# A DFT exchange through DRAM becomes a transposing DMA, for six of eight batches

## The chip, the cores and the metric

The kernel runs on one core of a Trainium2 chip. TensorE (PE, with its weight loads shown apart as PEld) multiplies, ScalarE (ACT) and VectorE (DVE) empty the PSUM banks and do the elementwise work, GpSimd (POOL) and SyncE (SP) issue most of the DMAs. The metric is the device time of one execution in microseconds (us), smaller being better. The kernel before takes 849.25 us, the median of three runs (849.11 to 849.75).

## The reference

Two steps follow each other. The first is a Fourier mixing layer, the second a two-layer network on every token:

```
x: (8, 3008, 256)                      # batch, sequence, dim
X  = rfft(x, axis=1)                   # along the sequence
Yr = Xr @ w_r - Xi @ w_i + b_r         # complex matmul over dim
Yi = Xr @ w_i + Xi @ w_r + b_i
Y  = sign(Y) * max(|Y| - 0.01, 0)      # real and imaginary part apart
y  = irfft(Y, n=3008, axis=1)
h  = y.reshape(24064, 256) @ w_in      # (256, 2048)
g  = s * max(h, 0)**2 + b
out = g @ w_out                        # (2048, 256), float32
```

## The kernel before, in words

The sequence length is factored as 3008 = 94 x 32 (n1 and n2). The Fourier transform is then two short transforms, both done as matmuls with tables: one over n1 (94 values in, 96 table columns out, table `A_t`), then one over n2 (32 values, table `F_t`) for pairs of n1-frequencies. The inverse goes the other way: `T_t` over n2, then `C_t` over n1.

Between the transform over n1 and the one over n2 the data must change its layout: the first has n1 on the partitions, the second wants (frequency, n2) on the partitions, 128 at a time. This is the first exchange. The inverse has a like one, the second exchange (`vd`, `vs`).

Work is cut into units, small pieces for each batch b:

- `s1_units(b)`: 16 units, the transform over n1. In each, one matmul with `A_t` as the weights (94 x 96) and 512 columns of `x16`, the batch's input in float16, moving (L549); one eviction of 96 x 512 to the tile `u` (L171 on ACT or L175 on DVE). After every fourth unit SP stores 384 KB to a DRAM tile `ud` (L556). After the last one SP issues four loads of 384 KB from `ud` into four tiles `us` (L563), now with the wanted layout.
- `s23_units(b)`: the transform over n2 from `us` (L585), the complex matmul (L600, L614), the threshold, the inverse over n2 (L644), a store of `v` to DRAM (`vd`, L653), and at the end two loads of 768 KB into the tiles `vs` (L660). On the way SP copies blocks inside a tile `ring` (L634), 40 DMAs a batch.
- `s4_units(b)`: 14 units, the inverse over n1 from `vs` (L697): in each up to five pairs of a weight load (96 x 128 of `vs`) and a matmul of 96 moving columns of `C_t`. The result `yt` is what the network reads.

The network is the main stream. Its tokens come in 48 tiles of up to 512, each with 16 slots. In a slot `first_mm` issues two matmuls of the tile with `w_in` (L748), ACT applies the relu (L755), DVE or ACT the square (L762, L759), and `second_mms` of the tile before follow with `w_out` (L819, about four matmuls of 256 columns a slot). Two blocks of 128 output rows share an `ost` buffer, filled by DVE (L829) and stored by SP; there are three such buffers.

`schedule(start, span, units)` spreads a batch's units over slots; the order in which the program emits them is the order of every engine's queue. With s0, s1, s2 the first slots of batches b-2, b-1 and b, `s1_units(b)` takes slots s0+40 to s1-8, `s23_units(b)` begins at s1+2, `s4_units(b)` takes s2-14 to s2-2. Batch 0 goes another way (`first_batch`), in which `first_mm` has no part yet: its transform over n1 has the data as weights and `A_t` moving, four pairs to a unit (L361), and needs no exchange. Batch 1 has its s1 units at the end of `first_batch`. The evictions are dealt to ACT and DVE by a running estimate of both loads (`evac`).

Buffers: `u` has three (`upool`), `us` five of a quarter of a batch each (`uspool`; the tables `F_c` and `F_2` of batch 0 use them first), `vs` two halves (`vspool`). `emit_load_x(b+1)` loads the next batch's input at slot s1+6 into the four `x16` buffers, once the s1 units have read the old one.

Of the kernel before, what the change touches and what calls it, by code (L numbers as in the profile page):

```python
# [9 lines left out]
F16 = mybir.dt.float16  # L10
# [4 lines left out]
P = 128  # L15
N1 = 94
N2 = 32
NPAIR = 24
# [78 lines left out]
def kernel(  # L97
# [13 lines left out]
    nc = tc.nc  # L111
    B, S, D = x.shape
# [35 lines left out]
    fpool = ctx.enter_context(tc.tile_pool(name="psf", bufs=2, space=bass.MemoryType.PSUM))  # L148
    dpool = ctx.enter_context(tc.tile_pool(name="dram", bufs=2, space=bass.MemoryType.DRAM))
    xpool = ctx.enter_context(tc.tile_pool(name="xp", bufs=4))  # L150
    upool = ctx.enter_context(tc.tile_pool(name="up", bufs=3))
    uspool = ctx.enter_context(tc.tile_pool(name="usp", bufs=5))
    xfpool = ctx.enter_context(tc.tile_pool(name="xfp", bufs=4))
    mpool = ctx.enter_context(tc.tile_pool(name="mp", bufs=2))
    vpool = ctx.enter_context(tc.tile_pool(name="vp", bufs=3))
    vspool = ctx.enter_context(tc.tile_pool(name="vsp", bufs=2))
    ypool = ctx.enter_context(tc.tile_pool(name="yp", bufs=2))
    tpool = ctx.enter_context(tc.tile_pool(name="tp", bufs=2))
    rpool = ctx.enter_context(tc.tile_pool(name="rp", bufs=3))
# [21 lines left out]
    def one_bank():  # L181
        return fpool.tile([P, 512], F32, name="psf", tag="psf")

    def other_bank():
        return apool.tile([P, 512], F32, name="psa", tag="psa")
# [43 lines left out]
    for r in (0, 64):  # L229
        for i, bv in enumerate((b_r, b_i)):  # L230
            nc.sync.dma_start(out=b_g[r : r + 1, i], in_=bv.unsqueeze(0))
    F_c = uspool.tile([P, H, 2, N2], F16, name="F_c", tag="us")
    F_2 = [uspool.tile([P, H, P], F16, name="F_2", tag="us") for _ in range(2)]
    b_h = cpool.tile([P, D], F16, name="b_h")
    nc.vector.memset(b_h, 0.0)

# [113 lines left out]
    def first_batch():  # L350
# [113 lines left out]
                ps.rearrange("p (k n) -> p n k", n=N2), 512,  # L464
            )

        for h in range(2):
            vs[(0, h)] = vspool.tile([96, HW, D], F16, name="vs", tag="vs")

        def turn(ec, k):  # L470
            ps = two_banks()
            for j in range(8):
                nc.tensor.matmul(
                    ps[0:96, j // 4, (j % 4) * P : (j % 4) * P + P],
                    vt[:, ec, 8 * k + j, :], eye_t, start=True, stop=True,
                )
            h, n = divmod(8 * k, HW)
            evac(
                vs[(0, h)][:, n : n + 8, ec * P : (ec + 1) * P],
                ps[0:96].rearrange("p h (j e) -> p (h j) e", e=P), 1024,  # L480
            )

# [2 lines left out]
        def last_dft(ec, n2):  # L485

            ps = [one_bank(), other_bank()]
            for j in range(8):
                h, k = divmod(n2 + j, HW)
                nc.tensor.matmul(  # L490
                    ps[j // 4][:, (j % 4) * 96 : (j % 4) * 96 + 96],
                    vs[(0, h)][:, k, ec * P : (ec + 1) * P], C_t,
                    start=True, stop=True,
                )
            for i in range(2):
                evac(
                    yt[:, ec, n2 + 4 * i : n2 + 4 * i + 4, :],
                    ps[i][:, 0:384].rearrange("p (j n) -> p j n", n=96), 384,
                )

        more = s1_units(1, True)

        def some(n):
            for _ in range(n):
# [31 lines left out]
        return more  # L536


    def s1_units(b, more_banks=False):

        ud = dpool.tile([96, N2, D], F16, name="ud", tag="ud")
        hold = {}

        def unit(i):
            c, j = divmod(2 * i, XCH)
            if j == 0:
                hold["u"] = upool.tile([P, XCH, D], F16, name="u", tag="u")
            ps = other_bank() if more_banks and i % 2 else one_bank()
            nc.tensor.matmul(  # L549
                ps[0:96, :], A_t[0:N1, :], x16[(b, c)][0:N1, j * D : (j + 2) * D],  # L550
                start=True, stop=True,
            )
            u = hold["u"]
            evac(u[0:96, j : j + 2, :], ps[0:96, :].rearrange("p (j d) -> p j d", j=2), 512)
            if j == XCH - 2:
                nc.sync.dma_start(  # L556
                    out=ud[:, c * XCH : (c + 1) * XCH, :], in_=u[0:96]
                )
            if i == N2 // 2 - 1:
                uv = ud.rearrange("k n d -> (k n) d").rearrange("(q p) d -> p q d", p=P)  # L560
                for q in range(4):
                    t = uspool.tile([P, 6, D], F16, name="us", tag="us")
                    nc.sync.dma_start(out=t, in_=uv[:, 6 * q : 6 * q + 6, :])  # L563
                    us[(b, q)] = t

        return [lambda i=i: unit(i) for i in range(N2 // 2)]

    def s23_units(b):
# [8 lines left out]
        def fwd_unit(i):  # L577

            bank = one_bank()
            ps = bank.rearrange("p (r c j k) -> p r c j k", r=2, c=DC, j=2)  # L580
            t = us[(b, i // 3)]
            for j in range(2):
                q = (2 * i + j) % 6
                for dc in range(DC):
                    nc.tensor.matmul(  # L585
                        ps[:, :, dc, j, :], t[:, q, dc * P : (dc + 1) * P],
                        F_t[:, 2 * i + j, :], start=True, stop=True,
                    )
            xt = xfpool.tile([P, 3, DC, P], F16, name="xf", tag="xf")
            evac(xt[:, 1:3].rearrange("p r c k -> p (r c k)"), bank, 512)  # L590
            nc.vector.tensor_tensor(out=xt[:, 0], in0=xt[:, 1], in1=xt[:, 2], op=ALU.add)
            load["dve"] += 0.25
            xf[i] = xt
# [46 lines left out]
        def inv_unit(i):  # L640
            ps = one_bank().rearrange("p (j e) -> p j e", j=2)
            z = zt.pop(i)
            for j in range(2):
                nc.tensor.matmul(  # L644
                    ps[:, j, :], T_t[:, 2 * i + j, :], z[:, j, :], start=True, stop=True
                )
            if i % 2 == 0:
                hold["v"] = vpool.tile([P, 4, D], F16, name="v", tag="v")
            v = hold["v"]
            h = 2 * (i % 2)  # L650
            evac(v[:, h : h + 2, :], ps, 512)
            if i % 2 == 1:
                nc.sync.dma_start(  # L653
                    out=vd[2 * i - 2 : 2 * i + 2].rearrange("q p e -> p q e"), in_=v
                )
            if i == H - 1:
                vv = vd.rearrange("q (k n) e -> (q k) (n e)", n=N2)
                for h in range(2):
                    t = vspool.tile([96, HW, D], F16, name="vs", tag="vs")
                    nc.sync.dma_start(  # L660
                        out=t.rearrange("k n e -> k (n e)"),
                        in_=vv[:, h * HW * D : (h + 1) * HW * D],
                    )
                    vs[(b, h)] = t

        units = []

# [14 lines left out]
    def s4_units(b):  # L682

        groups = []
        for lo in range(0, N2, 5):
            for ec in range(DC):
                groups.append((lo, min(5, N2 - lo), ec))

        def unit(g):
            n2, w, ec = groups[g]  # L690
            if g == 0:
                yts[b] = ypool.tile([P, DC, N2, 96], F16, name="yt", tag="yt")
            yt = yts[b]
            ps = one_bank()
            for j in range(w):
                h, k = divmod(n2 + j, HW)
                nc.tensor.matmul(  # L697
                    ps[:, j * 96 : (j + 1) * 96],
                    vs[(b, h)][:, k, ec * P : (ec + 1) * P], C_t,
                    start=True, stop=True,  # L700
                )
            evac(
                yt[:, ec, n2 : n2 + w, :],
                ps[:, 0 : w * 96].rearrange("p (j n) -> p j n", n=96), w * 96,
            )
            if g == len(groups) - 1 and b >= 2:
                pr, half = divmod(b, 2)
                if half == 0:
                    tails[pr] = tpool.tile([P, DC, 2, N2, 14], F16, name="tail", tag="tail")
                nc.gpsimd.tensor_copy(out=tails[pr][:, :, half], in_=yt[:, :, :, 80:94])  # L710

        return [lambda g=g: unit(g) for g in range(len(groups))]


# [127 lines left out]
    def schedule(start, span, units):  # L842
        for i, u in enumerate(units):
            plan.setdefault(start + (i * span) // len(units), []).append(u)
# [1 line left out]
    more = first_batch()  # L846
    load.update(act=0.0, dve=0.0)
    def load_x_2():
        emit_load_x(2, us[(1, 3)][0:1, 0, 0:1])

    mark = {}
    for i, tl in enumerate(tiles):
# [7 lines left out]
    for b in range(2, B):  # L860
        s0, s1, s2 = mark[b - 2], mark[b - 1], mark[b]
        p = s1 - s0
        schedule(s0 + 40, p - 48, s1_units(b))
        p = s2 - s1
        schedule(s1 + 2, p - 30, s23_units(b))
        schedule(s2 - 14, 12, s4_units(b))
        if b + 1 < B:
            plan.setdefault(s1 + 6, []).append(lambda b=b: emit_load_x(b + 1))
# [43 lines left out]
```

## Time and profile before

| what | value |
|---|---|
| time, median of three runs | 849.25 us |
| the profiled execution | 849.11 us |
| its span, first to last instruction | 847.2 us |
| TensorE clock granted | full in all slices |
| PE busy | 833.7 us, 98% |
| DVE busy | 691.5 us, 82% |
| ACT busy | 641.2 us, 76% |
| bytes moved by DMA | 96.06 MB, 113 GB/s |

The profile page gives busy time by engine, the span in 40 slices with the tenths of each that an engine was busy, the chain of work that ended last (followed back from the last instruction to what released it), and groups of instructions by line. In a group "out<-in" names the tiles, then come the shape, the count after "x", the busy time and the mean duration of one; behind the bar stands the idle time of the engine just before the group. A duration of a matmul holds its latency too, and matmuls overlap, so what one costs in a stream is read from the distance between starts in the timeline. Records of SP's queue are called SPq.

### The profile page before, as it was taken

How to read it: one execution, taken by the hardware profiler on the slowest of the kernel's cores; microseconds unless marked ns; L12 is line 12 of the kernel's file. 1: busy time of each engine (PE TensorE's matmuls, PEld its weight loads, DVE VectorE, ACT ScalarE, POOL GpSimd, SP SyncE). 2: the span in 40 equal slices, each digit the busy share in tenths (PEclk: the TensorE clock that was granted, in tenths of full speed). 3: DMA queues.
4: the chain of work that ended last, by engine and by line, in shares of the span. 5: the costliest groups of instructions: out<-in, count | busy, mean ns of one | idle time of the engine just before them, and what ended most of it. 6: DMA issues, size and time to landing. Idle time of an engine off the chain costs nothing.

```text
span 847.2 us, 17072 instructions
## 1 busy us (share of the span) xinstructions
PE 833.7 (98%) x6645; PEld 598.8 (71%) x6645; DVE 691.5 (82%) x1016; ACT 641.2 (76%) x854; POOL 45.6 (5%) x71
## 2 busy tenths in 40 slices
PE   7999999999999999999999999999999999999997
PEld 6757767777677766777677776777667777766765
DVE  5899987888878987888878888798977888776674
ACT  5888877787778877787777887787877777766673
POOL 4331000000000000000000000000000000000000
PEclk9999999999999999999999999999999999999999
DMA  8946467224762367324762248613354223411111
GB/s 200 173 131 139 118 160 192 78 70 108 193 161 60 99 157 191 95 79 108 179 173 57 73 105 202 170 41 91 101 156 120 61 79 98 112 33 39 38 44 50
DMA packets 105746, 96.06 MB, mean 113 GB/s; under 512 B 9542, under 2 KB 97482, under 8 KB 104322
## 3 DMA queue, kind: packets, MB, share of 16 engines
q1 hardware_dynamic: 99218, 80.55, 32.9%
q0 software_dynamic: 6448, 14.42, 10.5%
q8 instruction: 52, 0.85, 0.4%
q14 instruction: 28, 0.23, 0.1%
HBM read 53.52 MB, written 46.66 MB: 118 GB/s over the span
## 4 chain that ended last, share of the span: by engine, by line
PE 87%; DVE 4%; ACT 3%; DMA 3%; issue 2%; SPq 0%; POOL 0%; DVEq 0%; ACTq 0%; POOLq 0%
PE psa L819 36%; PE psh L748 35%; PE psf L614 4%; PE psf L549 2%; PE psf L600 2%; PE psf L585 2%; PE psf L644 2%; PE psf L697 2%; ACT rt L755 1%; DVE gt L762 1%; DMA out_dram<-ost 1%; DMA x<-in_x_dram 1%; DMA us<-ud 1%; DMA F_c<-dft_fwd 1%; PE psh L409 1%
## 5 line engine op out<-in xcount | busy, mean ns | idle before, releaser
L755 ACT ACTIVATE rt<-psh 128x1024 f32<-128x1024 f32 (+2 forms) x384 | 386.9, 1009 | 119.3 <-PE psh L748 117.9
L762 DVE TENSOR_TENSOR gt<-rt 128x1024 f16<-128x1024 f32 (+2 forms) x321 | 384.1, 1200 | 97.9 <-ACT rt L755 97.2
L819 PE MATMUL psa<-w_out_t,gt 128*128 128x256 f16 (+1 forms) x3024 | 454.3, 272 | 0.1
L819 PEld LDWEIGHTS <-gt 128*128 128x128 f16 (+1 forms) x3024 | 301.0, 101 | 187.2 <-issue 1.7
L748 PE MATMUL psh<-yt,w_in 128*128 128x512 f16 (+1 forms) x1344 | 396.7, 378 | 0.3 <-ACT rt L755 0.3
L748 PEld LDWEIGHTS <-w_in 128*128 128x128 f16 x1536 | 142.9, 98 | 27.4 <-issue 2.1
L829 DVE SCALAR_TENSOR_TENSOR ost<-psa,s_bc,bias_bc 128x512 f32<-128x512 f32 (+2 forms) x97 | 71.1, 733 | 8.3 <-PE psa L819 7.1
L759 ACT ACTIVATE gt<-rt 128x1024 f16<-128x1024 f32 (+2 forms) x63 | 66.2, 1051 | 1.0
L619 DVE TENSOR_TENSOR ring<-psf,s 128x512 f16<-128x512 f32 x84 | 57.6, 685 | 3.7 <-PE psf L614 3.1
L171 ACT CAST v<-psf 128x512 f16<-128x512 f32 x78 | 45.2, 581 | 18.8 <-PE psf L644 18.8
L171 ACT CAST xf<-psf 128x512 f16<-128x512 f32 x82 | 47.9, 585 | 10.9 <-PE psf L585 10.9
L171 ACT CAST u<-psf 96x512 f16<-96x512 f32 x77 | 44.6, 580 | 11.0 <-PE psf L549 10.7
L748 PE MATMUL psh<-tail,w_in 128*128 128x512 f16 (+1 forms) x192 | 52.1, 353 | 0.0
L614 PE MATMUL psf<-W_g,xf 128*128 128x256 f16 x336 | 50.4, 273 | 0.0
L171 ACT CAST yt<-psf 128x480 f16<-128x480 f32 (+2 forms) x75 | 38.1, 521 | 13.6 <-PE psf L697 13.6
L200 POOL DMA_DIRECT2D x<-in_x_dram x36 | 18.7, 526 | 429.7 <-PE psf L549 428.6
L549 PE MATMUL psf<-x,A_t 94*96 94x512 f16 x104 | 39.7, 381 | 1.7 <-ACT yt L171 0.5
L625 DVE TENSOR_TENSOR ring<-ring,high 128x512 f16<-128x512 f16 x84 | 35.5, 423 | 2.3
L626 DVE TENSOR_TENSOR ring<-ring 128x512 f16<-128x512 f16 x84 | 35.5, 423 | 1.9
L624 DVE TENSOR_TENSOR ring<-ring,low 128x512 f16<-128x512 f16 x84 | 35.4, 422 | 1.6
L614 PEld LDWEIGHTS <-xf 128*128 128x128 f16 x336 | 32.9, 98 | 3.8
L697 PE MATMUL psf<-C_t,vs 96*128 96x96 f16 x448 | 33.0, 205 | 0.1
(88 smaller groups left out, 489.4 us busy)
## 6 DMA issues: line engine op xcount, KB each, us to landing
out_dram<-ost SPq DMA_DIRECT2D x152, 128.0 KB
ud<-u SPq DMA_DIRECT2D x28, 384.0 KB
us<-ud SPq DMA_DIRECT2D x28, 384.0 KB
vd<-v SPq DMA_DIRECT2D x42, 256.0 KB
vs<-vd SPq DMA_DIRECT2D x14, 768.0 KB
x<-in_x_dram POOLq DMA_DIRECT2D x28, 376.0 KB, 6.8
ring<-ring SPq DMA_DIRECT2D x280, 32.0 KB
out_dram<-ost SPq DMA_DIRECT2D x16, 120.0 KB
```

The costliest lines, as they stand in the source:

```text
L171: return None, nc.scalar.copy(out=dst, in_=src)
L549: nc.tensor.matmul(ps[0:96, :], A_t[0:N1, :], x16[(b, c)][0:N1, j * D : (j + 2) * D], start=True, stop=True,)
L614: nc.tensor.matmul(ps[:, r, :], xt[:, 2 - r, dc], W_g[:, dc, r], start=(dc == 0), stop=(dc == DC - 1),)
L619: nc.vector.tensor_tensor(out=t, in0=ps, in1=hold[i // 2][:, i % 2].unsqueeze(1).to_broadcast([P, 2, D]), op=ALU.add,)
L625: nc.vector.tensor_tensor(out=m, in0=m, in1=high, op=ALU.min)
L697: nc.tensor.matmul(ps[:, j * 96 : (j + 1) * 96], vs[(b, h)][:, k, ec * P : (ec + 1) * P], C_t, start=True, stop=True,)
L748: nc.tensor.matmul(o, w_in_t[dc][:, mc * P : (mc + 1) * P], r, start=(dc == 0), stop=(dc == DC - 1),)
L755: nc.scalar.activation(out=rt[:, :, 0:w], in_=ps[:, :, 0:w], func=AF.Relu)
L759: nc.scalar.activation(out=gt[:, :, 0:w], in_=rt[:, :, 0:w], func=AF.Square)
L762: nc.vector.tensor_tensor(out=gt[:, :, 0:w], in0=rt[:, :, 0:w], in1=rt[:, :, 0:w], op=ALU.mult)
L819: nc.tensor.matmul(ps[0:size, h, :], gts[(ti, mc // 2)][:, mc % 2, sub * size : (sub + 1) * size], w_out_t[:, mc, :], start=(mc == 0), sto ...
L829: nc.vector.scalar_tensor_tensor(out=ost[0:size, 0:k], in0=ps[0:size, 0:k], scalar=s_bc[0:size], in1=bias_bc[0:size, 0:k], op0=ALU.mult, o ...
```

## The change

For batches 2 to 7 the first exchange no longer goes through DRAM.

- The unit of the transform over n1 (`unit_late`) takes the data as weights: four pairs of a weight load (94 x 128 of `x16`) and a matmul of 96 moving columns of `A_t`, all into one PSUM bank. There are 16 units as before, eight for each half of the 256 dims. The eviction is 128 x 384, written into `u` with runs of four elements.
- After each half SP issues one transposing DMA of 128 x 3072 float16 (768 KB), SBUF to SBUF, from `u` to `us`. The four stores to `ud` and four loads from it fall away for these batches.
- The units sit in slots s1-36 to s1-14, in place of s0+40 to s1-8. The first transposing DMA follows unit 7 at slot s1-27, the second follows unit 15 at s1-16. The first unit that reads `us` stays at s1+2. On SP's queue the first transpose comes right after the two `vs` loads of batch b-1.
- `us` is one tile for a batch, with one buffer, `u` too, `vs` one tile for both halves. Batch 1 keeps the way through DRAM with the same sizes. `F_c` and `F_2` become parts of one tile `first_c`.

By the count of rows on PE's queue there are 288 more pairs of weight load and matmul (48 in each of six batches); SP's queue has 36 DMAs fewer (eight less two, in six batches).

```diff
-    upool = ctx.enter_context(tc.tile_pool(name="up", bufs=3))
-    uspool = ctx.enter_context(tc.tile_pool(name="usp", bufs=5))
+    upool = ctx.enter_context(tc.tile_pool(name="up", bufs=1))
+    uspool = ctx.enter_context(tc.tile_pool(name="usp", bufs=1))
...
-    vspool = ctx.enter_context(tc.tile_pool(name="vsp", bufs=2))
+    vspool = ctx.enter_context(tc.tile_pool(name="vsp", bufs=1))
...
-    F_c = uspool.tile([P, H, 2, N2], F16, name="F_c", tag="us")
-    F_2 = [uspool.tile([P, H, P], F16, name="F_2", tag="us") for _ in range(2)]
+    first_c = uspool.tile([P, 5, H * 64], F16, name="first_c", tag="us")
+    F_c = first_c[:, 0].rearrange("p (q r k) -> p q r k", q=H, r=2)
...
+        def unit_late(i):
+            dc, g = divmod(i, N2 // 4)
+            if i == 0:
+                hold["u"] = upool.tile([P, DC, 96, N2], F16, name="u", tag="u")
+                us[b] = uspool.tile([P, NPAIR, D], F16, name="us", tag="us")
+            u = hold["u"]
+            c, h = divmod(g, 2)
+            ps = one_bank()
+            for j in range(4):
+                lo = (4 * h + j) * D + dc * P
+                nc.tensor.matmul(
+                    ps[:, j * 96 : j * 96 + 96], x16[(b, c)][0:N1, lo : lo + P],
+                    A_t[0:N1, :], start=True, stop=True,
+                )
+            evac(
+                u[:, dc, :, 4 * g : 4 * g + 4],
+                ps[:, 0:384].rearrange("p (n k) -> p k n", k=96), 384,
+            )
+            if g == N2 // 4 - 1:
+                nc.sync.dma_start(
+                    out=us[b][:, :, dc * P : (dc + 1) * P],
+                    in_=u[:, dc].rearrange("p k n -> p (k n)"),
+                    transpose=True,
+                )
...
-            t = us[(b, i // 3)]
...
-                        ps[:, :, dc, j, :], t[:, q, dc * P : (dc + 1) * P],
+                        ps[:, :, dc, j, :], us[b][:, 2 * i + j, dc * P : (dc + 1) * P],
...
+                t = vs[b] = vspool.tile([P, N2, D], F16, name="vs", tag="vs")
                 for h in range(2):
-                    t = vspool.tile([96, HW, D], F16, name="vs", tag="vs")
                     nc.sync.dma_start(
-                        out=t.rearrange("k n e -> k (n e)"),
+                        out=t[0:96, h * HW : h * HW + HW].rearrange("k n e -> k (n e)"),
...
-        schedule(s0 + 40, p - 48, s1_units(b))
+
+        schedule(s1 - 36, 22, s1_units(b))
```

More of the change, by code (lines that the diff above doesn't have):

```diff
@@ L231 @@
             nc.sync.dma_start(out=b_g[r : r + 1, i], in_=bv.unsqueeze(0))
-    F_c = uspool.tile([P, H, 2, N2], F16, name="F_c", tag="us")
-    F_2 = [uspool.tile([P, H, P], F16, name="F_2", tag="us") for _ in range(2)]
+    first_c = uspool.tile([P, 5, H * 64], F16, name="first_c", tag="us")
+    F_c = first_c[:, 0].rearrange("p (q r k) -> p q r k", q=H, r=2)
+    F_2 = [
+        first_c[:, 1 + 2 * i : 3 + 2 * i].rearrange("p s (q k) -> p (s q) k", k=P)
+        for i in range(2)
+    ]
     b_h = cpool.tile([P, D], F16, name="b_h")
@@ L465, in inv_dft @@
             )
-        for h in range(2):
-            vs[(0, h)] = vspool.tile([96, HW, D], F16, name="vs", tag="vs")
+        vs[0] = vspool.tile([P, N2, D], F16, name="vs", tag="vs")
         def turn(ec, k):
@@ L476, in turn @@
                 )
-            h, n = divmod(8 * k, HW)
             evac(
-                vs[(0, h)][:, n : n + 8, ec * P : (ec + 1) * P],
+                vs[0][0:96, 8 * k : 8 * k + 8, ec * P : (ec + 1) * P],
                 ps[0:96].rearrange("p h (j e) -> p (h j) e", e=P), 1024,
@@ L488, in last_dft @@
             for j in range(8):
-                h, k = divmod(n2 + j, HW)
                 nc.tensor.matmul(
                     ps[j // 4][:, (j % 4) * 96 : (j % 4) * 96 + 96],
-                    vs[(0, h)][:, k, ec * P : (ec + 1) * P], C_t,
+                    vs[0][0:96, n2 + j, ec * P : (ec + 1) * P], C_t,
                     start=True, stop=True,
@@ L499, in last_dft @@
                 )
-        more = s1_units(1, True)
+        more = s1_units(1, late=False)
         def some(n):
@@ L536, in first_batch, with s1_units @@
         return more
-    def s1_units(b, more_banks=False):
-        ud = dpool.tile([96, N2, D], F16, name="ud", tag="ud")
+    def s1_units(b, late=True):
         hold = {}
+        def unit_late(i):
[22 more added lines that the diff above has]
+                )
         def unit(i):
             c, j = divmod(2 * i, XCH)
-            if j == 0:
-                hold["u"] = upool.tile([P, XCH, D], F16, name="u", tag="u")
-            ps = other_bank() if more_banks and i % 2 else one_bank()
+            if i == 0:
+                hold["u"] = upool.tile([P, 3, XCH, D], F16, name="u1", tag="u")
+                hold["ud"] = dpool.tile([96, N2, D], F16, name="ud", tag="ud")
+            ps = other_bank() if i % 2 else one_bank()
             nc.tensor.matmul(
@@ L552, in unit @@
             )
-            u = hold["u"]
+            u, ud = hold["u"][:, c % 3], hold["ud"]
             evac(u[0:96, j : j + 2, :], ps[0:96, :].rearrange("p (j d) -> p j d", j=2), 512)
             if j == XCH - 2:
-                nc.sync.dma_start(
-                    out=ud[:, c * XCH : (c + 1) * XCH, :], in_=u[0:96]
-                )
+                nc.sync.dma_start(out=ud[:, c * XCH : (c + 1) * XCH, :], in_=u[0:96])
             if i == N2 // 2 - 1:
                 uv = ud.rearrange("k n d -> (k n) d").rearrange("(q p) d -> p q d", p=P)
+                us[b] = uspool.tile([P, NPAIR, D], F16, name="us", tag="us")
                 for q in range(4):
-                    t = uspool.tile([P, 6, D], F16, name="us", tag="us")
-                    nc.sync.dma_start(out=t, in_=uv[:, 6 * q : 6 * q + 6, :])
-                    us[(b, q)] = t
+                    nc.sync.dma_start(
+                        out=us[b][:, 6 * q : 6 * q + 6], in_=uv[:, 6 * q : 6 * q + 6, :]
+                    )
+        if late:
+            return [lambda i=i: unit_late(i) for i in range(N2 // 2)]
         return [lambda i=i: unit(i) for i in range(N2 // 2)]
@@ L580, in fwd_unit @@
             ps = bank.rearrange("p (r c j k) -> p r c j k", r=2, c=DC, j=2)
-            t = us[(b, i // 3)]
             for j in range(2):
-                q = (2 * i + j) % 6
                 for dc in range(DC):
                     nc.tensor.matmul(
-                        ps[:, :, dc, j, :], t[:, q, dc * P : (dc + 1) * P],
+                        ps[:, :, dc, j, :], us[b][:, 2 * i + j, dc * P : (dc + 1) * P],
                         F_t[:, 2 * i + j, :], start=True, stop=True,
@@ L657, in inv_unit @@
                 vv = vd.rearrange("q (k n) e -> (q k) (n e)", n=N2)
+                t = vs[b] = vspool.tile([P, N2, D], F16, name="vs", tag="vs")
                 for h in range(2):
-                    t = vspool.tile([96, HW, D], F16, name="vs", tag="vs")
                     nc.sync.dma_start(
-                        out=t.rearrange("k n e -> k (n e)"),
+                        out=t[0:96, h * HW : h * HW + HW].rearrange("k n e -> k (n e)"),
                         in_=vv[:, h * HW * D : (h + 1) * HW * D],
                     )
-                    vs[(b, h)] = t
         units = []
@@ L695, in unit @@
             for j in range(w):
-                h, k = divmod(n2 + j, HW)
                 nc.tensor.matmul(
                     ps[:, j * 96 : (j + 1) * 96],
-                    vs[(b, h)][:, k, ec * P : (ec + 1) * P], C_t,
+                    vs[b][0:96, n2 + j, ec * P : (ec + 1) * P], C_t,
                     start=True, stop=True,
@@ L848, in load_x_2 @@
     def load_x_2():
-        emit_load_x(2, us[(1, 3)][0:1, 0, 0:1])
+        emit_load_x(2, us[1][0:1, NPAIR - 1, 0:1])
     mark = {}
```

## The prediction

> **What bounds the kernel now.** I read the page from the top: busy times, slices, the chain, then the groups. The first two:
>
> ```profile
> PE 833.7 (98%) x6645; PEld 598.8 (71%) x6645; DVE 691.5 (82%) x1016; ACT 641.2 (76%) x854; POOL 45.6 (5%) x71
> ...
> PE   7999999999999999999999999999999999999997
> ...
> DVE  5899987888878987888878888798977888776674
> ACT  5888877787778877787777887787877777766673
> ...
> DMA  8946467224762367324762248613354223411111
> ...
> PE 87%; DVE 4%; ACT 3%; DMA 3%; issue 2%; SPq 0%; POOL 0%; DVEq 0%; ACTq 0%; POOLq 0%
> ```
>
> PE is full from the second slice to the last but one and carries 87% of the chain. DVE and ACT keep 10 to 30% free; DMA comes in humps. A busy PE is not proof that it sets the pace, since its ends are modelled, so I looked at a stretch of the timeline in the middle, columns start, duration, engine, line, instruction:
>
> ```profile
> 529.82 0.60 PE L819 MATMUL psa<-w_out_t,gt 128*128 128x256 f16 x4
> 530.26 0.59 PE L697 MATMUL psf<-C_t,vs 96*128 96x96 f16 x10
> 530.68 0.49 PE L748 MATMUL psh<-tail,w_in 128*128 128x384 f16 x2
> 531.01 0.27 PE L819 MATMUL psa<-w_out_t,gt 128*128 128x256 f16 x1
> 531.34 0.38 PE L549 MATMUL psf<-x,A_t 94*96 94x512 f16 x1
> 531.55 0.49 PE L819 MATMUL psa<-w_out_t,gt 128*128 128x256 f16 x3
> 531.88 0.38 PE L697 MATMUL psf<-C_t,vs 96*128 96x96 f16 x5
> 532.09 0.49 PE L748 MATMUL psh<-tail,w_in 128*128 128x384 f16 x2
> ```
>
> Every group starts where the columns of the one before run out: 4 x 256 columns take 0.44 us (529.82 to 530.26), 2 x 384 take 0.33. There is no gap: the columns that pass through PE set the time here, and one removed is time removed. Two prices stand in these lines. One L549 matmul of 512 columns occupies 0.21 to 0.22 us. Ten pairs of weight load and 96-column matmul (L697) occupy 0.42 us, five 0.21: 0.042 us a pair.
>
> The groups concerned, and two waits:
>
> ```profile
> L171 ACT CAST u<-psf 96x512 f16<-96x512 f32 x77 | 44.6, 580 | 11.0 <-PE psf L549 10.7
> L549 PE MATMUL psf<-x,A_t 94*96 94x512 f16 x104 | 39.7, 381 | 1.7 <-ACT yt L171 0.5
> L697 PE MATMUL psf<-C_t,vs 96*128 96x96 f16 x448 | 33.0, 205 | 0.1
> ```
>
> ```profile
> SPq L556 <- DVE u L175: 58.9, 10, 24.5
> SPq L660 <- DMA vd<-v: 21.1, 9, 5.0
> ```
>
> In all, PE waits 1.7 us ahead of L549 and 0.1 ahead of L697. SP is idle enough to sit 24.5 us in one wait; nobody pays for it. The exchange is hidden but for batch 1, whose `us` load is on the chain and is not changed.
>
> **What the skill says.** "TensorE: Matmul & The Clock Gate", section on loading the stationary operand (LDWEIGHTS): the time of a weight load goes with the columns, not the rows, and weights are pulled ahead of running matmuls. The trace agrees: a pair costs 0.042 us, about what 96 columns cost at L819's rate (0.44 us for 1024 columns is 0.041 for 96), so the weight load of 128 columns hides. Three pages price the transposing DMA, of which this trace has none: "Advanced Engine Details and Errata", section X-Bar Transpose (TRN2), calls it as fast as a regular DMA; "DMA: Bandwidth & Descriptors", section Latency and other measured facts, gives 261 GB/s for a non-contiguous case; "VectorE: DVE Perf Modes", section The three transpose paths, gives 1309 ns for one 128 x 128 block.
>
> **Part 1, PE.** Removed: 16 x 6 = 96 matmuls of 512 columns at 0.2175 us (elsewhere in the timeline two L748 matmuls of 512 columns take 0.43 to 0.44 us; half of that fits the 0.21 to 0.22) = 20.9 us. Added: 96 units of four pairs. At L697's 0.042 a unit is 0.17 us, 16.3 us in all. Batch 0 runs the same form: starts at L361 lie 0.19 and 0.17 us apart for four pairs. So a unit saves 0.03 to 0.05 us; I take 0.046, 4.4 us in all; both ends 2.7 and 4.8. The reason is plain: 512 columns used 96 output rows, 384 columns use 128.
>
> **Part 2, evictions.** 96 x 512 costs 580 ns on ACT and 682 on DVE; 128 x 384 with runs of four is in batch 0 (L361's evictions): 478 and 558. That frees about 10 us of ACT and DVE over 96 evictions. Worth nothing while PE sets the pace; at most the small stalls of one dense stretch at 290 to 310 us, where PE lost 0.53 us in two 10 us windows. I take 0, range 0 to 0.5 gained. The units are denser (16 in 22 slots instead of 32 to 48), but 14 s4 units in 12 slots already run through the same two `psf` banks with 0.1 us of wait. If that cover were gone each unit would pay up to one eviction's half us, 48 us in all; the s4 row speaks against it.
>
> **Part 3, DMAs removed.** 24 stores and 24 loads of 384 KB, with SP's issue time of 0.3 to 0.6 us each. All hidden before, so nothing gained; less traffic beside `vs` loads and output stores.
>
> **Part 4, the transposes.** Twelve of 768 KB. By 261 GB/s one takes 3.0 us; by 24 blocks of 1309 ns, one after the other, 31.4 us (estimates from the two pages). How long is allowed? In batch 5 of the kernel before, SP issues the `vs` loads at 416.1 us and PE first reads `us` at 444.8, 28.7 us later; the first transpose stands right behind those loads. The second is 18 slots ahead of the first use; 16 slots took 17.4 us there (444.76 less 427.33), so 19.6 us. If both run one after the other, PE waits once 2d is above about 28 us: d up to 14 us costs nothing. If the data of the first waits until the 1.5 MB of `vs` has landed, some 7.5 us at the 200 GB/s of the busy slices, d up to 10.5 us. I take 3 to 9 us, hidden.
>
> Queued behind the transposes on SP are the output stores, then the `ring` copies of the next s23 units, which begin after `us` is read. A store held back d us holds its `ost` buffer. A new `ost` comes every eight slots, 8.7 us; with three of them a buffer is wanted again 26 us after it is filled, and a store took 6.8 us on the chain at 131.8 us, so 19 us of delay hide; beyond, L829 stops DVE and the squares behind it. This limit comes later than the one of `us`. The input loads are on POOL's queue, not behind SP.
>
> **Part 5, buffers.** One `us` buffer: its last reader for batch b-1 is at slot s1-44 (228 for s1 = 272), the transpose at s1-27. One `u`: next written 60 slots after the second transpose. One `vs`: read until s1-2, loaded again near s2-28. `x16` is read until s1-14 instead of s1-8 and its load stays at s1+6. The memory of batch 0's tables is wanted by batch 1's `us` only after their last readers, as one of four quarters already was. All cost 0; the nearest margin is 17 slots.
>
> **Sum.** Profiled execution 849.1 us (span 847.2 and 1.9 around it) less 4.4 is 844.7; the median is 0.1 higher, so 844.8 us.
>
> **The rivals.** (A) The transposes are too slow. At d = 31.4 us both end 62.8 us after the first starts, with 28 us allowed: 35 us of PE idle in each of six batches, 210 us, about 1,055 us. It turns the sign at d of about 14.4 us (28 plus the 0.73 us that a batch gains, halved). For it: the 1309 ns[...]. Against: a block's 1309 ns holds a fixed latency (a plain 384 KB exchange load lands in 5.5 us on the chain), and two pages give bandwidths. Milder, d of 15 us: 2 us a batch, 12 less 4.4, 857.
> (B) The transposes are quick enough but the output stores behind them come late and DVE stalls for a few us in some batches: gain eaten, 848 to 852.
> (C) The weight loads do not hide, so that the unit costs as much as before: 849, no change. Against it the ten L697 pairs in 0.42 us.
> (D) DVE or ACT become the bound in the dense slots. in the table of 10 us windows DVE reaches 98% once; but it loses work.
>
> **How the numbers follow.** Hidden transposes and the PE gain: 0.72, with 843.3 to 846.5 for its own range (from the ends of parts 1 and 2). (C) and (D), with (B) where it eats just the gain: 0.06. (B) on the slower side: 0.07. (A): 0.15. About 0.2% (1.7 us) is what can be told from no change. Faster 0.72, same 0.06, slower 0.22. The range runs from 843 to 852, which leaves out (A) and little else.
>
> **What would show it.** Right: the new L556 group with 384 matmuls, four pairs 0.17 us apart; PE still at 98 to 99%; the first reads of `us` (L612) without a wait; transposes landing well ahead of slot s1+2. Wrong: PE idle ahead of L612 on the DMA into `us`, SP held for ten us or more by L565, L854 waiting for DMA `out_dram<-ost`, or a slot that takes longer than before where the late units run.

## The result, and the profile after

The changed kernel takes 893.61 us (median; 885.49 to 897.14), the kernel before 849.18 us beside it (849.03 to 849.75). The ratio is 1.0508 [1.0435, 1.0582]: 44 us slower, where 4 us faster was forecast. In three of the experiments below one run lay over 1.5% above the fastest of its kernel; such slow runs are left out of their times and ratios. The profiled execution took 895.01 us, with a span of 893.2 us.

The page of the changed kernel, its busy times, slices and chain:

```profile
PE 843.1 (94%) x6933; PEld 612.4 (69%) x6933; DVE 686.7 (77%) x1016; ACT 638.8 (72%) x854; POOL 45.8 (5%) x71
...
PE   8899997999958999899994999979999999999997
...
PEclk9999999999988999999997999989999999999999
DMA  8945469222992339423496223942336122411111
...
PE 80%; DMA 7%; DVE 7%; ACT 3%; issue 2%; SPq 1%; POOL 0%; DVEq 0%; ACTq 0%; POOLq 0%
```

PE's row has five holes (slices 7, 12, 17, 22 and 27), where the row before was full, and at three of them (12, 22 and 27) the granted clock drops too. In each hole, or in the slice before it, DMA is at 9. PE's share of the chain falls from 87 to 80%, and DMA's rises from 3 to 7%.

The two groups of PE that read `us` and `x16` (busy, mean ns, idle before), and two rows of the table of waits (total us, times, longest):

```profile
L612 PE MATMUL psf<-F_t,us 128*128 128x128 f16 x336 | 35.0, 227 | 35.9 <-DMA us<-u 35.7 <-DVE ring L646 0.2
L556 PE MATMUL psf<-A_t,x 94*128 94x96 f16 x384 | 32.2, 206 | 3.0 <-DVE u L175 1.7 <-DVE v L175 0.9 <-DVE ring L646 0.2
```

```profile
PE psf L612 <- DMA us<-u: 35.7, 8, 7.9
...
DVE ost L854 <- DMA out_dram<-ost: 23.2, 4, 8.9
```

PE waits 35.7 us for the transposed data. The idle times of all PE groups add up to 45.6 us, against 9.2 before: 36.4 more. PE's busy time is 9.4 us longer (843.1 less 833.7). Together that is 45.8 of the 46.0 us that the span grew. PE is busy longer although it has less to stream, because part of the time it runs at half clock, as shown below.

Batch 5 shows how the hole comes about. SP's timeline (start, duration, instruction; a row of several runs from the first start to the last end):

```profile
440.25 0.81 SPq L687 DMA_DIRECT2D vs<-vd  x2
441.36 15.07 SPq L565 DMA_TRANSPOSE us<-u  x1
456.48 17.32 SPq L806 DMA_DIRECT2D out_dram<-ost  x4
473.85 4.85 SPq L565 DMA_TRANSPOSE us<-u  x1
```

The first transpose holds SP for 15.07 us: its record on the queue lasts that long, and nothing behind it is issued meanwhile. The first output store behind it holds SP for 14.5 us more; the median of a store is 0.6. So the second transpose is issued 32.5 us after the first, and PE reads its data only at 481.48, 40 us after the first was issued.

The hold is not the whole delay. The trace also has every packet that the DMA engines moved; a transpose is 3072 packets of 256 bytes, and here it counts as landed when the last of them ends. The first transpose of batch 5 lands 33.3 us after its issue, which fits PE's first read of it at 475.30 (shown further down). In batches 2, 3, 4 and 6 it takes 22.5 to 31.6 us, and in batch 7, where no input is loaded, 9.7. The second transposes, issued when the loads are over, land after 5.9 to 8.0 us.

POOL's timeline in the same stretch, then in the same part of the kernel before:

```profile
443.41 0.52 POOL L200 DMA_DIRECT2D x<-in_x_dram  x1 [83.32 <-PE psf L556]
446.36 0.52 POOL L200 DMA_DIRECT2D x<-in_x_dram  x1 [2.43 <-PE psf L556]
448.45 0.52 POOL L200 DMA_DIRECT2D x<-in_x_dram  x1 [1.57 <-PE psf L556]
451.40 0.52 POOL L200 DMA_DIRECT2D x<-in_x_dram  x1 [2.44 <-PE psf L556]
```

```profile
407.36 0.52 POOL L200 DMA_DIRECT2D x<-in_x_dram  x1 [12.75 <-PE psf L549]
419.53 0.51 POOL L200 DMA_DIRECT2D x<-in_x_dram  x1 [11.66 <-PE psf L549]
432.22 0.51 POOL L200 DMA_DIRECT2D x<-in_x_dram  x1 [12.18 <-PE psf L549]
```

The program plans `emit_load_x(b+1)` for slot s1+6, behind the first read of `us`. POOL doesn't keep to that place: it has nothing else to do, and starts each load as soon as PE has read its `x16` buffer for the last time. In the kernel before, these last reads were 12 us apart. Now units 8 to 15 read the four buffers a second time in quick succession, so that all four loads start within 8 us, under the first transpose. In the window from 450 to 460 us the DMA engines are busy 1.38 times over by the profile and move 53 GB/s; over the whole kernel the median time of an input load from issue to landing rises from 6.8 to 13.4 us.

What the hole costs besides itself, in four rows of the timeline from 475 us on and a window of 6 us (span, PE, PEld, DVE, ACT, POOL busy, clock, DMA share, GB/s):

```profile
475.30 0.29 PE L612 MATMUL psf<-F_t,us 128*128 128x128 f16 x1 [5.48 <-DMA us<-u]
476.48 0.75 DVE L854 SCALAR_TENSOR_TENSOR ost<-psa,s_bc,bias_bc 128x512 f32<-128x512 f32 x1 [8.25 <-DMA out_dram<-ost]
481.48 0.50 PE L612 MATMUL psf<-F_t,us 128*128 128x128 f16 x3 [5.90 <-DMA us<-u]
...
481.78 1.06 PE L773 MATMUL psh<-yt,w_in 128*128 128x512 f16 x2
```

```profile
476.00:482.00 6.00, 0.52 (x4) 0.45 (x5) 3.02 (x3) 0.00 (x0) 0.00 (x0) 0.50 0.98 210
```

PE waits twice for `us`, DVE waits 8.25 us for an output buffer, and once PE goes on, its clock is 0.50: two L773 matmuls last 1.06 us instead of 0.59. The Trainium skill, "TensorE: Matmul & The Clock Gate", section Part 1: The HAM clock gate, states this: after an idle window of about 3.4 us the array runs at half rate until it has been busy for such a window. The trace agrees for the long waits: in batch 5 the clock falls 4.7 us after PE stops and is back 3.3 us after it goes on, and the five reduced stretches, one at each hole, last 3.4 to 13.7 us. It differs for the shortest hole: in batch 4 PE waited only 2.24 us (to 365.08), and its clock was still at 0.50 from 365.3 to 368.7 us. So a wait shorter than the page's window was enough here.

Batch 7, after which no input is loaded, is the control inside the same trace: its transposes hold SP for 8.05 and 4.65 us and PE does not wait for them.

### The profile page after: what moved, and what is told of

It is laid out like the page before. It is cut to its first block, busy times and chain, and to the rows that moved or that the text cites. A ratio compares the mean times of both kernels' runs of the same rounds, so it can differ in the third digit from the quotient of the medians.

```text
span 893.2 us, 17577 instructions
## 1 busy us (share of the span) xinstructions
PE 843.1 (94%) x6933; PEld 612.4 (69%) x6933; DVE 686.7 (77%) x1016; ACT 638.8 (72%) x854; POOL 45.8 (5%) x71
## 4 chain that ended last, share of the span: by engine, by line
PE 80%; DMA 7%; DVE 7%; ACT 3%; issue 2%; SPq 1%; POOL 0%; DVEq 0%; ACTq 0%; POOLq 0%
PE psa L844 33%; PE psh L773 32%; DMA us<-u 4%; PE psf L641 4%; DVE gt L787 2%; PE psf L612 2%; PE psf L722 2%; PE psf L627 2%; PE psf L556 2%; PE psf L671 2%; ACT rt L780 1%; DMA x<-in_x_dram 1%; DVE ring L646 1%; PE psh L413 1%; DMA us<-ud 1%
## 5 line engine op out<-in xcount | busy, mean ns | idle before, releaser
L787 DVE TENSOR_TENSOR gt<-rt 128x1024 f16<-128x1024 f32 (+2 forms) x318 | 379.8, 1198 | 97.7 <-ACT rt L780 97.0
L773 PE MATMUL psh<-yt,w_in 128*128 128x512 f16 (+1 forms) x1344 | 402.5, 382 | 0.3 <-ACT rt L780 0.3
L773 PEld LDWEIGHTS <-w_in 128*128 128x128 f16 x1536 | 138.2, 99 | 15.5 <-issue 1.3
L854 DVE SCALAR_TENSOR_TENSOR ost<-psa,s_bc,bias_bc 128x512 f32<-128x512 f32 (+2 forms) x97 | 71.1, 733 | 32.5 <-DMA out_dram<-ost 23.2
L784 ACT ACTIVATE gt<-rt 128x1024 f16<-128x1024 f32 (+2 forms) x66 | 69.2, 1049 | 1.1
L612 PE MATMUL psf<-F_t,us 128*128 128x128 f16 x336 | 35.0, 227 | 35.9 <-DMA us<-u 35.7
L171 ACT CAST v<-psf 128x512 f16<-128x512 f32 x80 | 46.7, 584 | 22.8 <-PE psf L671 22.6
L612 PEld LDWEIGHTS <-us 128*128 128x128 f16 x336 | 26.8, 102 | 39.8 <-DMA us<-u 37.4
L773 PE MATMUL psh<-tail,w_in 128*128 128x512 f16 (+1 forms) x192 | 52.1, 353 | 0.0
L618 DVE TENSOR_TENSOR xf<-xf 128x256 f16<-128x256 f16 x84 | 23.9, 287 | 33.7 <-ACT xf L171 33.5
L171 ACT CAST u<-psf 128x384 f16<-128x384 f32 (+1 forms) x78 | 37.7, 488 | 12.8 <-PE psf L556 12.2
L171 ACT CAST yt<-psf 128x480 f16<-128x480 f32 (+2 forms) x69 | 35.1, 524 | 13.5 <-PE psf L722 13.5
## 6 DMA issues: line engine op xcount, KB each, us to landing
x<-in_x_dram POOLq DMA_DIRECT2D x28, 376.0 KB, 13.4
```

What stands on the lines that cost most here:

```text
L171: return None, nc.scalar.copy(out=dst, in_=src)
L612: nc.tensor.matmul(ps[:, :, dc, j, :], us[b][:, 2 * i + j, dc * P : (dc + 1) * P], F_t[:, 2 * i + j, :], start=True, stop=True,)
L773: nc.tensor.matmul(o, w_in_t[dc][:, mc * P : (mc + 1) * P], r, start=(dc == 0), stop=(dc == DC - 1),)
L784: nc.scalar.activation(out=gt[:, :, 0:w], in_=rt[:, :, 0:w], func=AF.Square)
L787: nc.vector.tensor_tensor(out=gt[:, :, 0:w], in0=rt[:, :, 0:w], in1=rt[:, :, 0:w], op=ALU.mult)
L854: nc.vector.scalar_tensor_tensor(out=ost[0:size, 0:k], in0=ps[0:size, 0:k], scalar=s_bc[0:size], in1=bias_bc[0:size, 0:k], op0=ALU.mult, o ...
```

## The experiments

**Theory**: the input loads, started early by POOL, collide with the transposes. **Rivals**: the transposes are too slow by themselves (A of the prediction), the queue order on SP is at fault, or the gate on the loads would be a gain of its own.

### Loads held back behind the second transpose (e1_gate)

```diff
-            plan.setdefault(s1 + 6, []).append(lambda b=b: emit_load_x(b + 1))
+            plan.setdefault(s1 + 6, []).append(
+                lambda b=b: emit_load_x(b + 1, us[b][0:1, NPAIR - 1, D - 1 : D]))
```

`emit_load_x` can take a `first`: POOL copies that one element ahead of each load, so no load starts before the element has arrived. Here it is an element that the second transpose writes.

> The changed kernel, with one edit: the loads of the next batch's input wait, by a one-element copy on POOL, until the second transpose of this batch has landed. Theory (the loads on POOL's queue start as soon as the late units free the input buffers, right under the first transpose, and slow each other down): SP holds the first transpose for about 8 us in every batch as it does in batch 7, no wait ahead of L612, 843 to 847 us, 4 us faster than the kernel before. Rival 1 (the transposes are slow behind the vs loads, and batch 7 escapes for another reason): 880 us or more, first transposes still 15 us or longer. Rival 2 (the gain on PE is not there, the stall hides it): no stall, but 849 us or more.

848.0 us beside 849.75: 0.9981 [0.9973, 0.999]. One line of code takes back all of the 44 us. SP's timeline in batch 5 of this kernel:

```profile
415.19 7.93 SPq L565 DMA_TRANSPOSE us<-u  x1
423.17 3.59 SPq L806 DMA_DIRECT2D out_dram<-ost  x4
426.80 4.36 SPq L565 DMA_TRANSPOSE us<-u  x1
```

The second transpose is issued 11.6 us after the first instead of 32.5, and L612 no longer waits for `us`. Against the kernel with the loads ungated the PE groups are idle 34.8 us less and busy 12.3 us less, 47.1 together, for 46.8 us of span: the second figure is for the most part the price of the half clock. In the changed kernel PE is busy for 21.5 us while its clock is reduced, and half of that, an estimate of 10.7 us, is lost; 1 us more belongs to the start of the kernel. The first transposes of this kernel land 9.4 to 11.0 us after their issue, the second ones after 5.5 to 7.2. The gain, however, is 1.75 us and not 4.4, and the time lies 1 us above the range that I had given.

### The gate in the kernel before (e4_before_gate)

```diff
-            plan.setdefault(s1 + 6, []).append(lambda b=b: emit_load_x(b + 1))
+            plan.setdefault(s1 + 6, []).append(
+                lambda b=b: emit_load_x(b + 1, us[(b, 3)][0:1, 0, 0:1]))
```

> The kernel before with the same gate on the input loads, now behind its us loads from DRAM. Theory: input loads are hidden wherever they stand, 849 us within 1. If the gate itself brings time by sparing DMA humps: below 848.

849.57 us beside 849.75: 0.9997 [0.9989, 1.0006]. The gate alone is worth nothing; it matters only where something collides. Here, too, the four loads start within 2 us of each other (446.11 to 448.15 in batch 5), and no output store is held for more than 1.5 us: four loads together do no harm without a large copy in flight ahead of the stores.

### Plain copies in place of transposes (e2_plain)

```diff
-                    in_=u[:, dc].rearrange("p k n -> p (k n)"),
-                    transpose=True,
+                    in_=u[:, dc].rearrange("p (q k) n -> p q (k n)", k=4),
```

The same bytes between the same tiles, the loads ungated as in the changed kernel; the transposition is left out.

> The changed kernel with plain SBUF to SBUF copies of the same 768 KB in place of the transposes, so the layout change is left out; the input loads start as early as in the changed kernel. If any transfer of that size beside the input loads is enough to stall: 870 us or more. If it takes the transposing form: copies held by SP for less than 3 us each, no wait ahead of L612, 843 to 847 us.

848.23 us beside 849.75: 0.9979 [0.9971, 0.9987], and no wait for `us` (1.2 us above my range, like the gated kernel). SP's timeline, first rows of batch 5:

```profile
416.53 0.66 SPq L565 DMA_DIRECT2D us<-u  x1
...
417.67 10.92 SPq L805 DMA_DIRECT2D out_dram<-ost  x1
```

So it takes the transposing form to lose the time, but the second line forbids a simple story. The plain copy is off SP in 0.66 us, and the next store is held in its place: 10.4 to 14.2 us in batches 2 to 6, beside the input loads, and 7.2 us in batch 7, without them. The plain copy delays its queue as well, and the loads lengthen that: it lands 16.5 to 18.4 us after its issue beside the loads, and after 10.4 in batch 7. Alone, then, the two forms are alike (9.7 us for the transpose of batch 7); beside the same loads the transpose takes 22.5 to 33.3 us. The delay of the plain copy stays hidden: the second copy is issued 15 to 17 us after the first, where the second transpose comes 23 to 32.5 us after.

### Half of the loads held back (e3_half)

```diff
-            if first is not None:
+            if first is not None and (b == 2 or c >= 2):
```

together with the gate of the first experiment: two of four loads may start early.

> The changed kernel with only the last two of the four input loads of a batch behind the transposes. If the loss goes with the bytes that fly beside the transpose: the first transpose held for 10 to 16 us, 845 to 870 us. If one load is enough to spoil it: 880 us or more. If it takes the whole hump: as the full gate, 843 to 847.

867.0 us beside 849.75: 1.0185 [1.0158, 1.0212], 17 us lost where four loads lose 44. The first transposes hold SP for 16.0, 20.1, 14.8, 12.6 and 17.2 us in batches 2 to 6, and for 7.9 in batch 7; two of these are above the 10 to 16 that I had expected. They land 18.6 to 25.0 us after their issue. The table of waits:

```profile
PE psf L612 <- DMA us<-u: 13.2, 4, 5.9
```

A dose and an effect: the loss grows with the loads in flight.

### Smaller loads without a conversion (e9_nocast)

```diff
+    Z_d = nc.inline_tensor(np.zeros((N1, XCH * D), np.float16), name="other_x").ap()
...
-                    in_=xv[:, c * XCH * D + i * w : c * XCH * D + (i + 1) * w],
+                    in_=xv[:, c * XCH * D + i * w : c * XCH * D + (i + 1) * w]
+                    if b < 3 else Z_d,
```

The loads of batches 3 to 7 read a small float16 table, half the bytes and no conversion on the way; what is written, and the number of packets, stay. The result is computed from other data.

> The changed kernel without the gate, in which the input loads of batches 3 to 7 read a small float16 table in DRAM in place of the input, so they move half the bytes from DRAM and convert nothing; batches 3 to 7 are computed from other data. If a load from POOL's queue of any kind disturbs the transpose: first transposes 15 us or longer, 870 us or more. If it is the conversion or the bytes read: 10 us or less, below 852 us.

880.88 us beside 849.69: 1.0365 [1.033, 1.0401]. PE waits 20.1 us for `us`, and these loads land in 15.8 us (median), no sooner than the converting ones. My expectation of first transposes held for 15 us or longer came true in one batch of five (18.2 us; 8.2 to 13.0 in the others). Their data is late all the same, 22.6 to 26.1 us after the issue, so the hold alone is a poor measure of the delay. Neither the conversion nor the bytes read are needed for the collision: packets from POOL's queue of either kind disturb. Since 31 us are lost here and not 44, a part in the size of the loss is not excluded. The same loads issued from another queue were not run.

### The whole block twelve slots earlier (e5_early)

```diff
-        schedule(s1 - 36, 22, s1_units(b))
+        schedule(s1 - 48, 22, s1_units(b))
```

No gate. If only the time allowed to `us` were short, twelve slots more should mend it.

> The changed kernel without the gate, with the late units 12 slots earlier (s1-48 to s1-26); the input loads then start earlier too and still run under the first transpose. If all of the loss is that us comes late: first transposes still held 15 to 28 us, but no wait ahead of L612, 847 to 852 us. If the collision also costs through what waits behind the first transpose on SP (the vs loads and output stores now stand behind it): waits ahead of L722 or of L854 in its place, 855 to 880 us.

883.03 us beside 849.69: 1.0389 [1.0373, 1.0405]. `us` is in time now, and the loss turns up elsewhere. The table of waits:

```profile
PE psf L722 <- DMA vs<-vd: 21.6, 5, 5.9
```

At this place the input loads start between the two transposes (in batch 5 at 425.65 to 434.52 us, the transposes at 424.18 and 435.07), and the `vs` loads stand behind the second one on SP's queue (just ahead of it in batch 2). The `vs` loads are late, and PE waits for them instead, in batches 2 to 6; in batch 7, without input loads, it does not. My expectation that the first transposes would again hold 15 to 28 us was a miss: they took about 5, the second ones 8.3 to 10.8, and none landed later than 12.3 us after its issue. So here most of the delay falls on what stands last in the queue; an earlier place alone doesn't mend it.

### Loads let go under the second transpose (e12_second)

The gate of the first experiment, but on `us[b][0:1, NPAIR - 1, 0:1]`, which the first transpose writes.

> The gated kernel with the gate on the first transpose alone: the input loads now start when that one has landed and run under the second transpose, when the vs loads are over. If a transpose and the input loads disturb each other wherever they meet: the second transpose is held or lands later, waits ahead of L612, above 855 us. If the trouble takes the vs loads, the transpose and the input loads at once: within 1 us of the gated kernel, 847 to 849 us.

857.86 us beside 849.75 (851.7 to 860.45): 1.0107 [1.0087, 1.0127]. The profiled execution was the mildest, with 3.7 us of waits ahead of L612, and in it one second transpose is held long, in the timeline of SP in batch 5:

```profile
429.07 14.58 SPq L565 DMA_TRANSPOSE us<-u  x1
```

Its four input loads were issued at 428 to 430 us. With all of them behind it, it takes 4.36. The first transposes are at 7.7 to 9.2 again. The second ones land 7.2 to 16.1 us after their issue in batches 2 to 6, where those of the gated kernel take 5.5 to 7.2. So it doesn't take the first transpose, or `vs` loads just ahead of it: a second transpose is disturbed too where it meets the loads. The slower executions have no trace; that they lose their time in the same way is likely but not shown.

### Where the rest of the forecast gain went (e6_later, e10_one, e11_both)

With the gate, PE still waits 2.9 us ahead of L556, most of it for DVE's evictions. The next kernel adds to the gate:

```diff
-        schedule(s1 - 36, 22, s1_units(b))
+        schedule(s1 - 29, 20, s1_units(b))
```

> The gated kernel with the late units in slots s1-29 to s1-9, clear of the last units of the batch before. Theory (of the 4.4 us on PE about 2 us went into PE waiting ahead of L556 for a psf bank whose eviction stands behind the threshold's work on DVE): the wait ahead of L556 falls from 2.9 us to below 1, 846 to 847.5 us. Rival (the missing part lies elsewhere, or us comes late with 7 slots less): 848 us or more.

846.53 us beside 849.69: 0.9964 [0.9952, 0.9977]; the wait ahead of L556 falls to 1.3 us (I had expected less than 1), and the transposes hold SP for 3.6 to 6.7 us. The cleanest measure is the time from PE's first read of `us` in one batch to that in the next, read from the timeline:

| batches | before | gate (e1) | gate, s1-29 (e6) |
|---|---|---|---|
| 1 to 2 | 84.29 | 83.42 | 83.06 |
| 2 to 3 | 102.26 | 102.76 | 101.94 |
| 3 to 4 | 90.49 | 89.36 | 89.09 |
| 4 to 5 | 103.14 | 102.93 | 102.79 |
| 5 to 6 | 101.15 | 100.87 | 100.69 |
| 6 to 7 | 101.61 | 101.89 | 101.27 |
| sum | 582.94 | 581.23 | 578.84 |

All six blocks of new units lie in this stretch. They bring 4.10 us at their later place and 1.71 at the changed kernel's. Each column is one execution; the same sum in the two kernels below is 580.48 (e10, the changed kernel's place) and 578.78 (e11, the later one), so the second figure can also be 2.5. The whole executions gain less, 3.16 us at the later place by the medians: in its trace the part ahead of the stretch is 0.5 us longer than in the kernel before, and the part behind it 0.6 us, for reasons that I haven't followed.

The next one is the gate with batch 1 on the transposing way too:

```diff
-        more = s1_units(1, late=False)
+        more = s1_units(1)
...
-        emit_load_x(2, us[1][0:1, NPAIR - 1, 0:1])
+        emit_load_x(2, us[1][0:1, NPAIR - 1, D - 1 : D])
```

> The gated kernel with batch 1, too, on the transposing way. Its exchange through DRAM stands on the chain that ends last (2.96 us and 5.45 us of DMA); the transposes replace it. If they land sooner: 1 to 3 us less than the gated kernel, 845 to 847. If the first slots are bound by ACT anyway or the two halves come later: 848 us or more.

847.51 us beside 849.69: 0.9974 [0.9964, 0.9984]. That is 0.5 us beyond my range, and not to be told from the gate alone: the two intervals overlap.

Both edits and the gate together:

> The gate, the late units at s1-29 to s1-9, and batch 1 on the transposing way. If the savings of the two runs before add: 845.5 to 846.5 us, 3 to 4 us faster than the kernel before. If batch 1 brings nothing beside it: 846.5 to 847.5.

845.1 us (844.85 to 845.57) beside 849.75: 0.9943 [0.993, 0.9955]. That is 0.4 us below my range. This version beats both kernels, by 4.65 us and by 48.5. DVE's share of its chain is 2%, half of the 4 in the kernel before, and PE's is 93 instead of 87%. How much batch 1 brings is left open: 0.5 us by the runs at the first place, 1.4 at the later one, with overlapping intervals in both cases.

## Why the prediction was wrong

**The step that failed** is Part 5, in the sentence that `x16` "is read until s1-14 instead of s1-8 and its load stays at s1+6", with "All cost 0", and with it the remark in Part 4 that the input loads "are on POOL's queue, not behind SP". A slot is only a place in the program. POOL reaches the loads long before and waits for the buffers alone, so the last reads of `x16` set the start. The kernel before shows this: its loads at 407 to 432 us lie well ahead of slot s1+6, since the first read of `us`, planned for s1+2, is at 444.76. I read the code there, not POOL's rows. The diff had the second half: each `x16` buffer is now read twice, once for each half of d, so all four come free one after the other in units 8 to 15, just behind the first transpose. And being on another queue protects nobody. The Trainium skill says so in "DMA: Bandwidth & Descriptors", section Issuing engines are not separate DMA queues: all DMAs run on the same 16 engines. The trace agrees: loads from POOL's queue and transposes from SP's lengthen each other. From issue to landing a load takes 13.4 us by the median instead of 6.8, a first transpose 22.5 to 33.3 us instead of the 9.4 to 11.0 of the gated kernel.

**Part 1** was right: pairs cost what they should. In the gated kernel a unit starts at 415.49 and the next group at 415.66, 0.17 us, as worked out. The 4.4 us of gain are 4.10 in the stretch above once nothing else is in the way. Two ends of ranges were added up wrongly, without effect here: 96 units at 0.03 us are 2.9 us and not 2.7, and 849.2 less 4.8 and 0.5 is 843.9 and not 843.3.

**Part 2** was mis-sized at "0". At s1-36 with 22 slots the evictions are not fully covered: 2.4 us of the gain are missing in that stretch (4.10 less 1.71; 1.6 in e10's execution). PE's visible wait ahead of L556, 2.9 us against 1.3 at the later place, accounts for 1.6 of them; the rest I have not placed. The changed kernel itself shows the same wait, 3.0. That it comes from DVE being busy there with the rows of `ring` and the squares is argued from the timeline, not tested apart.

**Part 3** was not tested apart; no run here shows a gain or a cost of the removed DMAs.

**Part 4** was about right for transposes alone. "I take 3 to 9 us" stands against landings of 5.5 to 7.2 us for the second ones of the gated kernel and 9.4 to 11.0 for the first ones, which move no packet for their first 5.5 to 6.2 us (in batch 5 the packets of the `vs` loads still run then). At the later place all land within 5.0 to 8.4 us. The allowance was right too: 28.7 us forecast, 28.4 in the changed kernel, from the first transpose (441.36) to the hole (469.8). What was wrong is that d would be the same in company: there the first transposes took 22.5 to 33.3 us. In batch 5 it was 32.5 us from issue to issue, and the data of the second took 7.6 more.

**The rivals.** The symptoms of (A) came, PE idle ahead of L612 on `us<-u`, but not its cause: alone, the transposes are quick enough, as batch 7 and the gate show. The 1309 ns a block that spoke for (A) are far off: in the gated kernel 24 blocks landed within 11.0 us. That the collision brought d near the 31.4 us of (A) is chance. The waits of (B) came as well, 23.2 us of DVE waiting for output stores, as a part of the same jam. (C) fell with the 0.17 us. (D) holds in a small way: in the gated kernel DVE has 7% of the chain instead of 4, and 2.4 us of the gain are missing. No case had the transfers of two queues slow each other, and none had the half clock, about 11 us of the loss.

**What stays open**: why the two slow each other so much that the bytes moved fall to 53 GB/s. The runs show that it goes with the number of loads, not with the bytes they read, and that the transposing form suffers more than a plain copy of the same bytes. They don't show what happens between the packets, nor whether loads from a queue other than POOL's would do the same.

## What to carry to other kernels

A DMA starts when its buffer comes free and its engine gets there, not where the program plans it; on an idle engine, read its rows in the trace and ask what frees the buffer after the change. Before putting a large on-chip transpose into a queue, list what every other queue will have in flight in that stretch, and hold the loads back with a real dependency if they meet. Where PE comes to wait for more than some 2 us at a time, add the half clock afterwards to the price of the wait.

## What the hardware showed that I had not expected

- A transposing DMA of 768 KB from SBUF to SBUF holds its issuing queue for 3.6 to 9.5 us alone, and for 15 to 28 us beside four input loads. A plain copy of the same bytes is issued in 0.66 us, but the next DMA on the queue then is held for 7.2 us alone and 10.4 to 14.2 beside the loads.
- Alone, the transpose and the plain copy land alike, 9.7 and 10.4 us after issue in batch 7. Beside the same four loads the transpose takes 22.5 to 33.3 us and the plain copy 16.5 to 18.4.
- While they collide, a high share of busy DMA engines means little: 1.38 with 53 GB/s, against 1.05 with 230 GB/s in the gated kernel (415 to 425 us).
- Eight waits of PE, 35.7 us in all and none over 7.9, cost about 11 us more in slower matmuls. One wait of 2.24 us was enough for 3.4 us at half clock.
